# Attention with a routed FFN on one core: another order of the beginning, an earlier z load, larger merge groups and another order of the last FFNs

## The chip, the core and the metric

One core of a Trainium2 chip runs the whole program. The engines are TensorE (PE; its weight loads are PEld), VectorE (DVE), ScalarE (ACT), GpSimd (POOL) and SyncE (SP), which issues nearly all transfers. Each runs its own instructions in the order in which they are written, and waits where an input or a buffer is not free. The metric is the device time of one execution in microseconds, lower is better.

## The reference

Batch 8, sequence 3136, model width 256, width of z 64, FFN width 1024, capacity 128:

```python
scores = (1 / S) * np.matmul(z, z.transpose(0, 2, 1))
attn = np.maximum(scores, 0.0) ** 2
x = u * np.matmul(attn, v)
# then, for each batch b
scores = x[b] @ w_gate
top_idx = np.argpartition(-scores, capacity)[:capacity]
xe = x[b, top_idx]
ye = np.maximum(xe @ w1, 0.0) @ w2
out[b] = x[b]
out[b, top_idx] = xe + sigmoid(scores[top_idx])[:, None] * ye
```

All of it is in float32. The kernel writes each float32 operand of a matmul as a high part (rounded to float32r) and a low part (the rest), and adds the products that matter.

## The kernel before

**Tiles and slots.** The 3136 columns of a batch are cut into seven chunks, 0 to 6: five of 512 and the last two of 256 and 320. The rows are cut into 24 blocks of 128 and one of 64. A slot is one chunk with a pair of row blocks (the last slot of a chunk has the block of 64 alone), so a chunk has 13 slots and a batch 91. For slot k, `scores(k)` multiplies ZH and ZL (high and low part of z) by the chunk's Z tile on PE into one of two score banks; ACT makes relu and its square, which gives the high part `hi`; DVE multiplies score and relu to `a` (L413), or ACT squares again; `low(k)` subtracts for the low part `lo` on POOL or DVE (L459). `mix(k)` multiplies V by hi (8 matmuls) and by lo (4 matmuls) into the accumulators. In the middle of mix(k), at matmul `turn`, the scores of slot k + LEAD (3) are issued. As attn is symmetric, squares of later row blocks are transposed on DVE and stored, and later chunks fetch them (`fetch`, `old_scores`) instead of computing them.

**Preparation.** `stage_z` and `stage_v` issue loads on SP, `prep_z` and `prep_v` split what has landed into high part (ACT) and low part; `bring_z` fills the chunk's Z tile. In `prep_v` the low part is always POOL's. For the batches after the first, z of a whole chunk is loaded into the one `zst` buffer two slots ahead of its `prep_z`, during the batch before.

**Order.** There is one order written out by hand: the loop over slots runs what `plan` holds for the slot, then mix, then the posts of the slot's tasks. What is chosen between engines goes by sums: `spend` adds an estimate to `busy` of an engine, and each slot takes a fixed amount off. `start()` stands ahead of slot 0: ten warm-up matmuls, loads, prep_z of chunk 0, then scores and prep_v for three slots, with prep_z of chunk 1 ahead of the third.

**The routed FFN.** After a batch, `route` and `choose` find the 128 best tokens and `expert` runs the FFN. Two batches' FFNs (5 and 6, in `held`) are put off to the end. In the last batch the choice is made from chunks 0 to 2, and `merge(b, c)` then merges chunks 3 to 6 into it one by one: the scores of the chunk are spread into rows (`spread`, `seen`), `keep_old` and `rank_old` rank the old choice, `count_old` and `count_new` count who beats whom (DVE, L827 and L829), `pick` makes a one-hot matrix and `what`, and `find` multiplies them on PE (L888). `keep_choice` then keeps the new choice for the next merge. A task is a list of PE operations that are placed in the mix of a slot, a post that follows, and a number of slots that the next task has to wait; a task without PE operations may go with the one before it into a slot. What is left after the last slot is run in a final list, with `held` and the last batch's FFN.

Of the kernel before, what the change touches and what calls it, by code (L numbers as in the profile page):

```python
# [40 lines left out]
def constants(S, cap):  # L41
# [25 lines left out]
    for i, (c0, w) in enumerate(chunks_of(S)[-LATE:]):  # L67
        t = c0 + w // 4 * np.arange(4)[None, :] + np.arange(P)[:, None]
        tok[:, i, :, 0] = t // Q * Q
        tok[:, i, :, 1] = t % Q  # L70
# [10 lines left out]
def attention_then_routed_ffn(ctx: ExitStack, tc: tile.TileContext, zt, ut, v, wg, w1, w2, cst, cst16, keys, outs, at, cap):  # L81
# [129 lines left out]
    def stage_z(b, i, n=None):  # L211
# [6 lines left out]
        for h in range(2):  # L218
            nc.sync.dma_start(st[h * 64 : h * 64 + 64, :n], zt[b, :, a : a + n])
        staged["z", b, i] = st  # L220

# [13 lines left out]
    def bring_z(b, c):  # L235
# [3 lines left out]
        for rows, z in ((slice(0, 64), ZH), (slice(64, P), ZL)):  # L239
            if b == 0 and c == 0:  # L240
                nc.scalar.copy(t[rows], z[rows, c0 : c0 + w].bitcast(F32))
# [11 lines left out]
    def stage_v(b, g):  # L253

        st = stage.tile([P, GT, D], F32, name="vst", tag="vst")
        if g < NJ // GT:
            for f in range(GT):
                src = v[b, g * CH + f * P : g * CH + (f + 1) * P, :].rearrange("(t a) d -> a t d", a=Q)
                nc.sync.dma_start(st[f * Q : (f + 1) * Q], src)
# [5 lines left out]
    def prep_v(b, g):  # L265
# [8 lines left out]
        split(src, *[t[:, w].rearrange("p h (f i) -> p h f i", i=Q) for w in range(2)], lo_on=nc.gpsimd.tensor_tensor)  # L274
        for q in range(n):
            V[b, 2 * g + q] = t[:, :, :, q * P : (q + 1) * P]
        spend(act=0.6, pool=1.3)
# [190 lines left out]
    def mix(k, beside, between):  # L468
# [14 lines left out]
        else:  # L483
# [7 lines left out]
            if first:  # L491
                todo.sort(key=lambda x: x[0])
        turn = 6 if first else 4 if last or len(slots[min(k + 1, len(slots) - 1)][2]) == 1 else 8
# [86 lines left out]

    def scores_of(b, c, xT):
# [3 lines left out]
        T4 = w // 4  # L585
        row = moe.tile([P, P + CH], F32, name="row", tag="hl", bufs=2)[:, : P + w]
        col = moe.tile([P, 4], F32, name="col", tag="col", bufs=2)[:T4]
# [8 lines left out]
        def seen(q):  # L596
            if q == 0:
                nc.scalar.copy(row[:, P:], bank[0])
            for i in range(2 * q, 2 * q + 2):
                junk = moe.tile([P, P], F32, name="own", tag="diag", bufs=2)[:T4, :T4]  # L600
                nc.vector.scalar_tensor_tensor(
                    junk, bank[0][:T4, i * T4 : (i + 1) * T4], 1.0, consts["ident"][:T4, :T4],
                    op0=ALU.mult, op1=ALU.mult, accum_out=col[:, i : i + 1],
# [210 lines left out]
    def merge(b, c):  # L814
# [5 lines left out]
        T4 = CHUNKS[c][1] // 4  # L820
# [15 lines left out]
        def keep_old():  # L836
            cnt["o"] = moe.tile([P, 3], F32, name="cnt_o", tag="cnt_o")
            cnt["n"] = moe.tile([P, 4, 3], F32, name="cnt_n", tag="cnt_n")
            cnt["rk"] = moe.tile([P, 5], F32, name="rk5", tag="rk5")
# [11 lines left out]
        def count_new(i, q):  # L851
            s, o = col[:, i : i + 1], P + i * T4
            to = cnt["n"][:T4, i]
            if q == 0:
                count(to[:, 0:1], row[:T4, P - n : o], s, ALU.is_ge)
            else:
                count(to[:, 1:2], row[:T4, o:], s, ALU.is_gt)
                count(to[:, 2:3], row[:T4, o : o + T4], s, ALU.is_equal, consts["before"][:T4, :T4])

        def pick():  # L860
            rk = cnt["rk"]
            nc.vector.tensor_reduce(rk[:T4, :4], cnt["n"][:T4], axis=AX.X, op=ALU.add)
# [391 lines left out]
```

## Time and profile before

| | us |
|---|---|
| median of 3 runs | 2184.3 |
| lowest and highest | 2183.02 and 2185.05 |
| the profiled execution | 2176.7 |
| its span, first to last instruction | 2174.4 |

| engine | busy us | share of the span |
|---|---|---|
| PE | 2111.9 | 97% |
| PEld | 1761.7 | 81% |
| DVE | 1532.7 | 70% |
| POOL | 1328.4 | 61% |
| ACT | 1219.2 | 56% |

The mean granted clock of PE over the span is 0.993 of full speed. A row of a timeline gives start, duration, engine, line, operation, output and inputs, how many instructions it merges, and in brackets how long the engine had been idle and what ended that.

### The profile page before, as it was taken

How to read it: one execution, taken by the hardware profiler on the slowest of the kernel's cores; microseconds unless marked ns; L12 is line 12 of the kernel's file. 1: busy time of each engine (PE TensorE's matmuls, PEld its weight loads, DVE VectorE, ACT ScalarE, POOL GpSimd, SP SyncE). 2: the span in 40 equal slices, each digit the busy share in tenths (PEclk: the TensorE clock that was granted, in tenths of full speed). 3: DMA queues.
4: the chain of work that ended last, by engine and by line, in shares of the span. 5: the costliest groups of instructions: out<-in, count | busy, mean ns of one | idle time of the engine just before them, and what ended most of it. 6: DMA issues, size and time to landing. Idle time of an engine off the chain costs nothing. (4 is left out here: it accounts for less than half of the span.)

```text
span 2174.4 us, 31815 instructions
## 1 busy us (share of the span) xinstructions
PE 2111.9 (97%) x10593; PEld 1761.7 (81%) x10593; DVE 1532.7 (70%) x2340; ACT 1219.2 (56%) x1489; POOL 1328.4 (61%) x691
## 2 busy tenths in 40 slices
PE   7899999999999999999999999999999999999987
PEld 5777888888888798887988889887888889887776
DVE  6656678765777667776677756777577775877785
ACT  5555476544765457654576546654466554765432
POOL 5675476664766557664576655865576665766351
PEclk8999999999999999999999999999999999999998
DMA  4779666787767876678767877678777787757850
GB/s 134 199 227 250 196 189 189 189 215 225 199 178 185 226 222 180 186 198 219 217 185 194 198 209 226 179 200 194 226 204 203 180 205 189 205 163 184 215 158 28
DMA packets 432467, 422.25 MB, mean 194 GB/s; under 512 B 150064, under 2 KB 341040, under 8 KB 428592
## 3 DMA queue, kind: packets, MB, share of 16 engines
q1 hardware_dynamic: 431536, 418.13, 70.8%
q0 software_dynamic: 768, 2.10, 0.4%
q8 instruction: 83, 1.36, 0.3%
q14 instruction: 80, 0.66, 0.1%
HBM read 235.29 MB, written 172.23 MB: 187 GB/s over the span
## 5 line engine op out<-in xcount | busy, mean ns | idle before, releaser
L498 PE MATMUL acc<-hi,V 128*128 128x512 f32 (+2 forms) x5376 | 1236.8, 368 | 7.6 <-ACT hi L372 2.7
L459 POOL TENSOR_TENSOR lo<-a,hi 128x1024 fp32r<-128x1024 f32 (+2 forms) x325 | 750.7, 2312 | 637.0 <-DVE a L413 512.0
L498 PEld LDWEIGHTS acc<-hi,V 128*128 128x128 f32 x5376 | 936.5, 189 | 171.1 <-DVE ut L543 7.8
L498 PE MATMUL acc<-lo,V 128*128 128x512 f32 (+2 forms) x2688 | 670.5, 366 | 15.6 <-POOL lo L459 15.3
L402 ACT ACTIVATE a<-sc 128x1024 f32<-128x1024 f32 (+4 forms) x408 | 362.8, 889 | 521.2 <-PE sc L392 405.0
L498 PEld LDWEIGHTS acc<-lo,V 128*128 128x128 f32 x2688 | 473.9, 189 | 104.8 <-POOL lo L459 23.6
L413 DVE TENSOR_TENSOR a<-sc,a 128x1024 f32<-128x1024 f32 (+2 forms) x330 | 335.0, 1015 | 302.4 <-ACT hi L403 270.8
L428 DVE STREAM_TRANSPOSE aT<-a 128x512 f32<-128x512 f32 (+1 forms) x520 | 341.2, 691 | 101.5 <-ACT a L408 56.4
L372 ACT CAST hi<-qk 128x1024 fp32r<-128x1024 f32 (+2 forms) x320 | 274.2, 861 | 242.7 <-PE acc L498 179.3
L403 ACT ACTIVATE hi<-a 128x1024 fp32r<-128x1024 f32 (+4 forms) x408 | 377.3, 925 | 22.1 <-PE acc L498 4.9
L459 DVE TENSOR_TENSOR lo<-qk,hi 128x1024 fp32r<-128x1024 f32 (+2 forms) x222 | 297.7, 1349 | 87.2 <-ACT hi L372 86.0
L392 PE MATMUL sc<-Z,ZL 128*128 128x512 f32 (+2 forms) x760 | 285.2, 379 | 6.7 <-DVE ZL L117 6.6
L392 PE MATMUL sc<-Z,ZH 128*128 128x512 f32 (+2 forms) x760 | 283.0, 376 | 6.9 <-ACT ZH L116 4.0
L459 POOL TENSOR_TENSOR lo<-qk,hi 128x1024 fp32r<-128x1024 f32 (+2 forms) x98 | 186.1, 1902 | 68.5 <-DVE lo L459 22.4
L392 PEld LDWEIGHTS sc<-Z,ZL 128*128 128x128 f32 x760 | 143.2, 188 | 38.8 <-DVE ZL L117 8.8
L392 PEld LDWEIGHTS sc<-Z,ZH 128*128 128x128 f32 x760 | 143.4, 189 | 36.1 <-ACT ZH L116 5.2
L117 POOL TENSOR_TENSOR V<-vst,V 128x512 fp32r<-128x512 f32 x96 | 132.2, 1384 | 33.4 <-ACT V L116 27.5
L563 POOL TENSOR_TENSOR ut<-x,w_run 128x1024 f32<-128x1024 f32 (+2 forms) x52 | 127.6, 2453 | 24.5 <-DVE x L554 22.5
L117 POOL TENSOR_TENSOR ZL<-zst,ZH 128x512 fp32r<-128x512 f32 (+2 forms) x56 | 67.4, 1208 | 36.7 <-ACT ZH L116 36.7
L116 ACT CAST V<-vst 128x512 fp32r<-128x512 f32 x96 | 58.3, 608 | 44.5 <-DMA vst<-in_v 44.5
L408 ACT ACTIVATE a<-a 128x1024 f32<-128x1024 f32 (+1 forms) x78 | 81.7, 1047 | 2.5
L543 DVE SCALAR_TENSOR_TENSOR ut<-acc,ut 128x512 f32<-128x512 f32 (+2 forms) x112 | 64.0, 613 | 9.6 <-PE acc L498 9.3
(138 smaller groups left out, 1050.9 us busy)
## 6 DMA issues: line engine op xcount, KB each, us to landing
squares<-aT SPq DMA_DIRECT2D x160, 512.0 KB, 3.5
qk<-squares SPq DMA_DIRECT2D x320, 256.0 KB, 5.9
squares_narrow<-aT SPq DMA_DIRECT2D x320, 128.0 KB, 3.7
qk<-squares_narrow SPq DMA_DIRECT2D x80, 512.0 KB, 4.9
vst<-in_v SPq DMA_DIRECT2D x192, 128.0 KB, 3.2
ut<-in_ut SPq DMA_DIRECT2D x40, 512.0 KB, 5.5
out<-x SPq DMA_DIRECT2D x160, 128.0 KB, 3.4
squares_own<-aT SPq DMA_DIRECT2D x39, 256.0 KB, 2.1
```

Source lines behind the costliest of these rows:

```text
L117: (lo_on or nc.vector.tensor_tensor)(lo, src, hi.bitcast(F32), op=ALU.subtract)
L372: nc.scalar.copy(by(hi), src)
L392: nc.tensor.matmul(ps[:, q], z[:, j * P : (j + 1) * P], mov, start=start, stop=not start)
L402: nc.scalar.activation(a, ps[:, :n], AF.Relu)
L403: nc.scalar.activation(pieces[0][0](hi), pieces[0][1], AF.Square)
L408: nc.scalar.activation(a, a, AF.Square)
L413: square = lambda: nc.vector.tensor_tensor(a[rows], ps[rows, :n], a[rows], op=ALU.mult)
L428: nc.vector.transpose(to, a[rows, q].rearrange("p (m t a) -> p m t a", t=GT, a=Q))
L459: on.tensor_tensor(view(lo), src, view(hi).bitcast(F32), op=ALU.subtract)
L498: nc.tensor.matmul(ac[h], w, mov, start=first and h not in started, stop=stop)
L543: nc.vector.scalar_tensor_tensor(xT[:, h, :w], acc[b, c][h], SCALE * SCALE, xT[:, h, :w], op0=ALU.mult, op1=ALU.mult)
L563: nc.gpsimd.tensor_tensor(wx, runs, consts["wg_run"].rearrange("p (o r) -> p o r", o=1).broadcast_to([P, NB, RUN]), op=ALU.mult,)
```

## The change

- `start()`: an early one-column copy on ACT; V of the first two slots is loaded by four DMAs that ACT issues; z of chunk 1 is loaded alone, chunks 2 and 3 behind V of the next slots (`more_z`), chunk 4 and the rest in slots 1 and 2. prep_z of chunk 1 stands ahead of all scores. Only slots 0 and 1 are scored ahead of mix(0); slots 2 and 3 are scored in it after three matmuls. The first V is split on DVE alone. Three warm-up matmuls become two.
- `bring_z` of the first chunk fills both halves of Z from the staged z, one by a copy on ACT, one by a subtraction on DVE.
- `prep_v` in the first batch puts the low part on DVE where POOL's sum is higher. V loads from the fourth on go two slots ahead of their use instead of three.
- In the later batches z of the five whole chunks is loaded five slots ahead instead of two.
- `merge` and `scores_of` work by groups of up to 128 tokens instead of a quarter of the chunk: two groups instead of four in chunk 5 (256), three in chunk 6 (320), four as before in chunks 3 and 4. `pick` rests two slots instead of one.
- The final list is in another order: the choice so far and the spread first, then the merge blended with the kept FFNs, with `find` behind them; one kept FFN is finished and the other's low parts are made while the gather runs, and the other's last matmuls and scatter go into the last FFN.

The diff, cut to its core:

```diff
 def bring_z(b, c):
             if b == 0 and c == 0:
-                nc.scalar.copy(t[rows], z[rows, c0 : c0 + w].bitcast(F32))
+                src, to = (by_rows(x, 0, CH)[rows] for x in (z, t))
+                st = staged["z", 0, 0][rows].rearrange("p (f t a) -> p f t a", t=GT, a=Q)
+                if z is ZH:
+                    nc.scalar.copy(to, st)
+                else:
+                    nc.vector.tensor_tensor(to, st, by_rows(ZH, 0, CH)[rows].bitcast(F32), op=ALU.subtract)
...
-    def prep_v(b, g):
+    def prep_v(b, g, on=None):
...
-        split(src, *[...], lo_on=nc.gpsimd.tensor_tensor)
+        lo_on, took = on or nc.gpsimd, {"dve": 1.0} if on else {"act": 0.6, "pool": 1.3}
+        if not on and b == 0 and busy["pool"] + 1.3 > busy["dve"] + 0.6:
+            lo_on, took = nc.vector, {"act": 0.6, "dve": 0.6}
+        split(src, *parts_of, on and on.tensor_copy, lo_on.tensor_tensor)
...
-        spend(act=0.6, pool=1.3)
+        spend(**took)
...
-            if first:
+            if first and (b or c):
                 todo.sort(key=lambda x: x[0])
-        turn = 6 if first else 4 if last or ...
+        turn = (6 if b or c else 3) if first else 4 if last or ...
...
 def merge(b, c):
-        T4 = CHUNKS[c][1] // 4
+        groups = groups_of(CHUNKS[c][1])
+        NG4 = len(groups)
...
-            *[([], [lambda i=i, q=q: count_new(i, q) for q in range(2)]) for i in range(4)],
-            ([], pick, 1),
+            *[([], [lambda i=i, q=q: count_new(i, q) for q in range(2)]) for i in range(NG4)],
+            ([], pick, 2),
             ([find], (lambda: keep_choice(st)) if more else None),
...
-                at_slots(k, lambda b=b, i=i: stage_z(b, i), use, 0.6)
+                at_slots(k, lambda b=b, i=i: stage_z(b, i), use, 0.6, lead=5 if i < WHOLE else 2)
...
 def start():
         warm(10)
         stage_z(0, 0)
-        stage_v(0, 0)
-        stage_z(0, 1, (WHOLE - 1) * CH)
-        stage_z(0, WHOLE, S + 64 - WHOLE * CH)
+        first = moe.tile([P, 1], F32, name="g", tag="g", bufs=2)
+        nc.scalar.copy(first, idle[0][:, :1])
+        stage_v(0, 0, nc.scalar)
+        stage_z(0, 1, (WHOLE - 1) * CH, CH)
+        stage_v(0, 1)
+        more_z(0, 2, 1)
+        more_z(0, 3, 1)
         prep_z(0, 0)
         bring_z(0, 0)
-        stage_v(0, 1)
-        for k in range(LEAD):
-            if k == LEAD - 1:
-                prep_z(0, 1)
-            more_scores(k)
-            settle_scores()
-            prep_v(0, k)
-        warm(3)
+        prep_z(0, 1)
+        more_scores(0)
+        prep_v(0, 0, nc.vector)
+        busy["pool"] = 3.0
+        settle_scores()
+        more_scores(1)
+        prep_v(0, 1)
+        settle_scores()
+        prep_z(0, 2, 1)
+        warm(2)
         stage_v(0, 2)
...
         held.reverse()
-        run(blend(rest, [t for i in (0, 2, 4) for f, _ in held for t in f[i : i + 2]]))
+        run(rest[:2])
+        *rest, find = rest[2:]
+        (f0, s0), (f1, s1) = held
+        run([*blend(rest, [*f0[:2], *f1[:2], *f0[2:4], *f1[2:4], *f0[4:]]), find])
         order.enter_context(tc.manual_schedule())
-        rest = first[:2] + [t for i in (0, 2) for _, f in held for t in f[i : i + 2]] + first[3:] + ffn + more
+        rest = [*first[:2], *f1[4:], *s0, *s1[:2], *first[3:], *ffn, *s1[2:], *more]
     run(rest)
```

## Rows read from the trace of the kernel before

**Rows 1.** Busy time by stretch: us of PE, PEld, DVE, ACT, POOL; PEclk; DMA share, GB/s.
```profile
10.00:20.00 10.00, 2.63 (x5) 1.22 (x5) 6.31 (x4) 4.75 (x7) 5.78 (x3) 0.50 0.44 102
...
40.00:60.00 20.00, 19.48 (x84) 15.29 (x83) 19.28 (x20) 14.64 (x20) 15.85 (x9) 1.00 0.59 176
...
800.00:1200.00 400.00, 396.98 (x1959) 332.09 (x1958) 294.14 (x441) 240.71 (x289) 264.71 (x136) 1.00 0.73 198
...
2120.00:2140.00 20.00, 14.54 (x88) 14.20 (x87) 15.60 (x66) 5.35 (x9) 6.68 (x5) 0.83 0.08 32
```

**Rows 2.** Waits of PE, whole run: us in total, times, longest us.
```profile
PE ids L888 <- DVE what L747: 8.5, 3, 4.4
```

**Rows 3.** Timeline of the beginning: start us, us, engine, operation, idle time and its releaser.
```profile
2.01 2.00 SPq L259 DMA_DIRECT2D vst<-in_v  x4
...
4.54 1.28 ACT L116 ACT_TABLE_LOAD   x1 [4.54 <-DMA zst<-in_zt]
...
5.83 0.62 ACT L116 CAST ZH<-zst 128x512 fp32r<-128x512 f32 x1
...
6.48 0.69 DVE L117 TENSOR_TENSOR ZL<-zst,ZH 128x512 fp32r<-128x512 f32 x1 [5.34 <-ACT ZH L116]
...
10.21 1.06 ACT L403 ACTIVATE hi<-a 128x1024 fp32r<-128x1024 f32 x1
...
11.29 1.23 DVE L413 TENSOR_TENSOR a<-sc,a 128x1024 f32<-128x1024 f32 x1 [4.12 <-ACT hi L403]
...
14.86 0.79 PE L392 MATMUL sc<-Z,ZH 128*128 128x512 f32 x1 [4.04 <-ACT ZH L116]
...
18.99 0.79 PE L392 MATMUL sc<-Z,ZL 128*128 128x512 f32 x1 [3.33 <-DVE ZL L117]
...
32.88 1.98 PE L498 MATMUL acc<-hi,V 128*128 128x512 f32 x8
...
36.56 1.99 PE L498 MATMUL acc<-hi,V 128*128 128x512 f32 x8
```

**Rows 4.** The same timeline: subtractions on DVE, and POOL's work beside one of them.
```profile
14.93 3.45 POOL L117 TENSOR_TENSOR V<-vst,V 128x512 fp32r<-128x512 f32 x2
...
17.19 1.74 DVE L117 TENSOR_TENSOR ZL<-qk,ZH 128x512 fp32r<-128x512 f32 x1
...
41.14 1.18 DVE L459 TENSOR_TENSOR lo<-a,hi 128x1024 fp32r<-128x1024 f32 x1
```

**Rows 5.** Timeline of the second batch and of the third: staged z.
```profile
483.02 1.21 SPq L219 DMA_DIRECT2D zst<-in_zt  x2
...
493.57 0.62 ACT L116 CAST ZH<-zst 128x512 fp32r<-128x512 f32 x1 [7.93 <-DMA zst<-in_zt]
...
496.31 2.14 PE L498 MATMUL acc<-hi,V 128*128 128x512 f32 x8 [1.25 <-ACT hi L403]
...
500.08 1.19 PE L498 MATMUL acc<-lo,V 128*128 128x512 f32 x4 [1.63 <-POOL lo L459]
...
762.14 1.21 PE L498 MATMUL acc<-lo,V 128*128 128x512 f32 x4 [1.66 <-POOL lo L459]
```

**Rows 6.** Timeline of the last 50 us: merges of the last chunks and the FFN.
```profile
2127.05 0.25 PE L888 MATMUL ids<-what,oh 128*128 128x5 bf16 x4 [4.39 <-DVE what L747]
...
2132.89 0.33 DVE L827 TENSOR_SCALAR_CACHE_REDUCE beats<-row,col 64x128 bf16<-64x128 f32 x1
...
2138.06 0.27 DVE L829 SCALAR_TENSOR_TENSOR beats<-row,col,c_sb 64x64 bf16<-64x64 f32 x1
...
2149.46 0.24 DVE L601 SCALAR_TENSOR_TENSOR own<-spread,c_sb 80x80 f32<-80x80 f32 x1 [4.13 <-ACT row L598]
...
2156.75 0.26 PE L888 MATMUL ids<-c,oh 80*128 80x2 bf16 x4
...
2158.90 2.04 PE L1010 MATMUL y<-ZH,hl 128*128 128x256 f32 x16
...
2162.35 0.73 PE L966 MATMUL h<-wh,xh 128*128 128x512 f32 x2 [1.19 <-ACT xh L116]
```

## What I expect of the change

> **What bounds the kernel now.** I read four views in this order: busy time by stretch, the waits of TensorE (PE), the timeline of the first 45 us, the timeline of the last 75 us. From 800 to 1200 us PE is busy 396.98 of 400 us at full clock; from 10 to 20 us it is busy 2.63 us of 10 at a granted clock of 0.50, and from 2120 to 2140 us 14.54 of 20 at 0.83 [rows 1]. So the middle is bound by PE's own matmuls, which this change leaves alone; time is to be had where PE waits: the beginning, single stalls in the middle, and the end. Each of these is a chain through other engines, and I cost each stretch on its own. A microsecond that PE no longer waits counts fully, as what follows is PE's own work.
>
> The beginning: PE waits 4.04 us for ZH of chunk 1 at 14.86 and 3.33 us for its ZL at 18.99, and the eight first matmuls of mix(2) begin at 32.88 [rows 3]. From there a slot takes 36.56 - 32.88 = 3.68 us, PE's pace. mix(2) is therefore my mark: where it stands after the change is the gain of the beginning. The middle: ScalarE (ACT) waits 7.93 us for the staged z at 493.57, and PE then loses 1.63 us at 500.08 for a low part from GpSimd (POOL) [rows 5]. The end: PE waits for `what` of the merge in three places, 8.5 us together [rows 2], one of them 4.39 us at 2127.05 [rows 6]. There the bound is the chain of the merges on VectorE (DVE): each merge needs the choice of the one before.
>
> **Part 1, the beginning.** The activation table is loaded at 4.54, only when z has landed, and takes 1.28; ZH follows at 5.83 [rows 3]. The new one-column copy takes the load to about 1.2 (when the zero tile is written), so ACT is free at 2.6. Then ACT issues the four loads of V(0): no row shows ACT issuing a DMA; SP needs 2.00 us for the same four [rows 3], and I take 0.5 each (0.1 would do no harm, 1.0 would put ZH at 6.6, later than now). So ACT is free at 4.6 and ZH begins there, 1.2 us earlier. ZL is 0.69 on DVE with POOL idle [rows 3]; the other half of Z is a second such subtraction instead of a copy on ACT. Scores of slot 0 begin near 6.7 and end at 7.7.
>
> The row shows the next cast right at the end of the 1.28 us load, with no gap [rows 3]. The Trainium skill (ScalarE: Activation LUTs, What ACT_TABLE_LOAD costs) adds a drain of 1.38 us to each load; by it ACT would be free at 4.0, ZH would begin at 6.0 and the beginning would gain about 1.4 us less.
>
> Then, with the durations of the rows: two ACT passes of about 1.05 each give hi(0) at 9.8; the product on DVE, 1.23, ends at 11.1 [rows 3]; lo(0) is now on DVE, 1.18 with POOL idle [rows 4], and ends at 12.3. hi(1) is ready at 11.9 and its product at 13.5. PE does three matmuls of mix(0) at 10, scores(2) at 11.1 when the first score bank is free, scores(3) at 13.6 when the second is. z of chunk 1 is a load of its own now and prep_z(0,1) stands ahead of all scores, so the waits of 4.04 and 3.33 us go. From 13.6 PE has 4 + 9 + 16 matmuls up to the end of mix(1): at 3.68/16 = 0.23 us each 6.7 us, to 20.3; if the first 3 to 4 us run at the 0.50 clock that the stretch shows now, 22. mix(2) also needs the low half of V(2). Adding up `spend` by the new rule puts V 2, 3, 5, 6, 10, 11 and 12 on DVE, 1, 4, 7, 8 and 9 on POOL, and all lo but lo(0) on POOL. V(2) stands on DVE behind the products and transposes of slots 2 and 3, and ends at 22 to 23. I put mix(2) at 23.4: a gain of 9.5. The lower bound is mix(2) at 27, if every DVE subtraction meets POOL (1.74 instead of 0.69, [rows 4]): gain 6; the upper is 21, full clock and no contention: gain 12. The later V loads (two slots ahead of their use instead of three) cost nothing: SP now waits with them for the buffer anyway, and two slots are 7.4 us; if that cover fails, a slot waits once for a load.
>
> **Part 2, z five slots in advance.** The load at 483.02 stands behind the two weight copies of the slot on SP's queue; the cast waits for it until 493.57 [rows 5]. Three slots more are about 8 to 11 us, which takes the two z DMAs ahead of those copies, at the price of two issues of 0.6 us in front of a store that no one waits for then. The buffer has been free since the chunk before, over seven slots. The same stall of 1.6 to 1.7 us stands in four passes (500.08, 762.14 and two more, at 1024 and 1287), and in the first PE loses another 1.25 at 496.31; in the fifth pass it is 0.2, in the sixth nothing. Sum 1.63 + 1.25 + 3 x 1.66 + 0.2 = 8.1, of which [rows 5] hold the first two passes. I take 7: what the stalls hide may come up next, such as a Z chunk behind the same copies. Bounds: 8.1, and 3 if ACT finds another late input there.
>
> **Part 3, the end.** Two edits meet. `pick` now rests two slots, so one more slot of PE work, about 1.8 us, stands ahead of each find; PE uses its wait for it. But each find of chunks 3 and 4 comes one slot later, so the merge of chunk 5 begins at slot 9 of the last chunk and not 7, and its find falls out of the loop into the final list. I worked this out from the rule that pops tasks: spread_old with count_old, two groups, two groups, pick, rest, find; and the order now (find at the ends of slots 1, 6, 11) follows from it. The DVE chain sets those times, so the finds of chunks 3 and 4 stay where they are, the second at 2127. For chunk 5 the counts of four groups run from 2132.89 to 2138.3 [rows 6], 1.3 us each with what lies between; two groups fewer save 2.6, of which the spread at the end of slot 9 and pick behind the last scaling on DVE take 0.6: gain 2.0. Then the scores of the last chunk: now DVE waits 4.13 us at 2149.46 for the copy that stands on ACT behind two rectifications [rows 6]. In the new order `seen` comes at once, but spread_old then stands behind twelve hidden matmuls on PE, 12 x 0.23 = 2.8 less 0.5 of DVE's own work, a wait of 2.3: gain 1.8. One group fewer there, with wider rows than in chunk 5: 1.5. The find that now runs at 2156.75 would come at about 2151.4.
>
> Behind it, 2156.75 to the first hidden matmul of the last FFN at 2162.35 is 5.6 us [rows 6]. The kept low parts and one scatter now stand in DVE's order before the gate: later by 0.4. The second kept FFN's last eight matmuls, 2.04/16 = 0.13 each [rows 6], stand between hidden and transposes: 1.0, of which PE's short waits give back 0.2. Net gain of the end 5.3 - 1.2 = 4.1; bounds 0 (the saved waits all come back) and 9 (PE stays at full clock, where it is at 0.83 now).
>
> **Sum.** 9.5 + 7 + 4.1 = 20.6 us. The profiled execution took 2176.7, span 2174.4 plus 2.3 around it; so 2156 for that one. The median of the runs shown is 7.6 above it, and the saving is the same: 2184.3 - 20.6 = 2163.7, rounded 2164. The bounds of the parts alone: gains of 9 to 29.
>
> **The rivals.** *The first batch becomes DVE's.* Eight subtractions more stand on DVE. DVE is busy 19.28 of 20 us from 40 to 60 us already [rows 1]. Beside POOL a 128x512 subtraction took 1.74 instead of 0.69: it began at 17.19 while POOL worked on its pair until 18.38, and ended 0.55 us behind it [rows 4]. If each moved one pays 1.74 or more, 8 x 1.74 = 14 us less one lo of 1.18 come to an engine with 0.04 of its time free: the gain of the beginning would be given back by the end of chunk 0, time 2173. A rule speaks for it: the Trainium skill (SBUF — State Buffer, Who interferes with whom) says that a DVE operation with two SBUF inputs and a POOL operation that reads SBUF exclude each other for a whole instruction. Against it: with all lo on POOL, DVE and POOL fall into turns, and LEAD of three slots, 11 us, covers single blocks. Chance 0.15.
>
> *The end doesn't gain.* The find of chunk 5, out of the loop, and the extra eight matmuls cost what the groups save: 2168; if the final list serialises on DVE, 3 us worse still, 2171. Chance 0.15.
>
> *The z load doesn't do what it says*: it lands earlier, but ACT then waits at the same place for another transfer behind the weight copies, as all of them queue there. 2171. Chance 0.08.
>
> *Slower: the clock.* PE begins early but with holes between 8 and 14 us, and stays at 1.2 GHz while DVE feeds it. Every us at the low level on PE's own work costs 0.5 us, so the low stretch would have to last 41 us longer than now to cancel the 20.6, through most of chunk 0; if it lasts to the end of that chunk near 75 us, 25 us are lost and the time is about 2189. Now the clock rises once PE has had unbroken work from 18.99 on, so I give it 0.05.
>
> **How the numbers follow.** The forecast has 0.57; these four have 0.15, 0.15, 0.08 and 0.05 and none is left over for a gain past the bounds. Range 2155 (all parts at their upper bounds) to 2176 (start given back and one more part failing). A measurement of this kernel tells about 0.2%, 4.4 us, from no change. Faster by more: forecast and the first three rivals, less the cases in which two of them meet: 0.89. Within: 0.06. Slower by more: the clock, 0.05.
>
> **What would show it.** Right: mix(2) near 23, scores beginning before 7, no waits for ZH or ZL of chunk 1; ACT's waits for the staged z gone and PE without the 1.66 us stalls; the last find near 2151 in the old count less 16.5. Wrong: a first load on ACT ending past 6; DVE subtractions of 1.7 us in a row in chunk 0 and PE waiting for V's low half; a granted clock of 0.5 beyond 25 us; a find of the last chunk that keeps its distance from the last mix.

## The result and the profile after

| | before | after |
|---|---|---|
| median beside each other, us | 2183.66 (4 runs) | 2152.88 (4 runs, 2149.70 to 2156.27) |
| ratio, 95% interval | | 0.986, 0.9838 to 0.9883 |
| profiled execution, us | 2176.7 | 2153.18 |
| its span, us; mean granted clock | 2174.4; 0.993 | 2151.4; 0.993 |

The change gains 30.8 us by the medians; 20.6 were forecast, and 2152.88 lies 2.1 us below the lower end of the range. The two profiled executions are only 23.5 us apart: the one of before lies 7.0 us below its median, the one of after 0.3 above. These 7.3 us are most of the 10.2 by which the forecast missed on the medians.

Where the 23 us of span lie, I read with marks: a mark is the begin of the first scaling of the accumulators on DVE (`ut<-acc`, L543 before, L559 after) at the end of a chunk. (7,4) is the mark at the end of chunk 4 of the last batch; "chunk 4 lost" sums, over batches 1 to 5, what chunk 4 takes beyond 36.06 us, its length in every kernel with the early load.

| stretch, us | before | after | gain |
|---|---|---|---|
| to the end of chunk 0 of batch 0 | 80.09 | 70.25 | 9.8 |
| rest of batch 0 | 214.88 | 211.80 | 3.1 |
| chunk 4 of batches 1 to 5, lost | 10.56 | 0.04 | 10.5 |
| the other chunks up to (7,4) | 1589.65 | 1587.58 | 2.1 |
| from (7,4) to the last instruction | 98.92 | 101.43 | -2.5 |

These are one execution of each. In after_again (below) the changed kernel has 70.04, 216.30, 0.04, 1586.69 and 100.90 in the same rows: the gains of chunk 0 and of chunk 4 come again, the 3.1 us of the rest of batch 0 do not.

The beginning, timeline of after, which answers to [rows 3]: start us, us, engine, operation, idle time and its releaser.

```profile
0.74 1.28 ACT L1178 ACT_TABLE_LOAD   x1 [0.74 <-PEq L1284]
1.18 0.88 ACTq L271 DMA_DIRECT2D vst<-in_v  x2
2.03 0.19 ACT L1178 CAST g<-zero 128x1 f32<-128x1 bf16 x1
3.87 2.72 ACTq L271 DMA_DIRECT2D vst<-in_v  x2
6.63 0.62 ACT L116 CAST ZH<-zst 128x512 fp32r<-128x512 f32 x1 [4.40 <-DMA qk<-in_zt]
8.82 0.76 PE L408 MATMUL sc<-Z,ZH 128*128 128x512 f32 x1 [3.18 <-DVE Z L253]
23.09 2.48 DVE L444 STREAM_TRANSPOSE aT<-a 128x512 f32<-128x512 f32 x4
23.52 0.39 PE L514 MATMUL acc<-hi,V 128*128 128x512 f32 x1
25.50 1.34 DVE L117 TENSOR_TENSOR V<-vst,V 128x512 fp32r<-128x512 f32 x2
26.29 2.82 PE L514 MATMUL acc<-hi,V 128*128 128x512 f32 x7 [2.38 <-DVE V L117]
```

The row at 3.87 merges two issues. A timeline that begins at 4.30 shows the second alone:

```profile
6.27 0.32 ACTq L271 DMA_DIRECT2D vst<-in_v  x1
```

The table is loaded at once, and the four issues on ACT last only 0.32 to 0.46 us each. But ACT waits ahead of the third and of the fourth, and ZH begins at 6.63, later than before. In the trace each of the two takes up the semaphore that told of the landing of an earlier load of z, and begins when that load has landed: the third 0.03 us after the first load of chunk 0 (3.84), the fourth 0.02 us after the first load of chunk 1 (6.25). mix(2) has its first matmul at 23.52 and goes on only at 26.29, because V's low part stands on DVE behind four transposes. In between there are no long holes: PE is busy 8.61 of 10 us from 10 to 20 us, against 2.63 [rows 1].

```profile
10.00:20.00 10.00, 8.61 (x30) 5.60 (x29) 6.69 (x7) 7.34 (x9) 4.39 (x3) 1.00 0.32 84
20.00:30.00 10.00, 7.62 (x27) 5.79 (x27) 7.93 (x11) 5.96 (x8) 5.70 (x3) 0.85 0.53 164
```

(Stretches of after: us of PE, PEld, DVE, ACT, POOL; granted clock; DMA share, GB/s.)

The 1.00 of the first row does not fit after's own matmuls: until 12.4 a score matmul lasts 0.63 us, from 14.66 on 0.40. In after_again the 0.63 us stand beside a granted clock of 0.50, so I take it that the first 3.6 us of PE's own work ran at the lower level in after too.

```profile
11.51 0.63 PE L408 MATMUL sc<-Z,ZH 128*128 128x512 f32 x1
14.66 0.40 PE L408 MATMUL sc<-Z,ZL 128*128 128x512 f32 x1
```
```profile
10.33 0.63 PE L408 MATMUL sc<-Z,ZH 128*128 128x512 f32 x1
10.00:12.00 2.00, 2.00 (x6) 1.24 (x4) 1.12 (x2) 1.40 (x2) 0.00 (x0) 0.50 0.58 135
```

(First after, then after_again. From 27 to 30 us the granted clock of after is 0.50 again.)

The middle, which answers to [rows 5]: the waits of PE over the whole run, in us, times, longest, first of before and then of after.

```profile
PE acc L498 <- POOL lo L459: 15.3, 16, 2.5
PE acc L498 <- DVE hi L462: 3.8, 3, 3.5
PE acc L498 <- ACT hi L372: 2.7, 3, 1.4
PE acc L498 <- ACT hi L403: 1.2, 1, 1.2
```
```profile
PE acc L514 <- POOL lo L475: 7.2, 12, 1.9
PE ids L916 <- DVE what L770: 6.3, 3, 3.7
PE acc L514 <- DVE V L117: 2.4, 1, 2.4
```

PE's waits for POOL's low parts halve, ACT no longer waits for a staged z of a later batch (before 41.9 us in 12 waits), and the 3.45 us that PE waited for `hi` at 75.50, the end of chunk 0, are gone.

The end of after, which answers to [rows 2, 6], in its timeline:

```profile
2109.14 0.75 PE L514 MATMUL acc<-hi,Vr 128*128 128x320 f32 x4
2113.58 0.21 PE L916 MATMUL ids<-what,oh 128*128 128x5 bf16 x2 [3.69 <-DVE what L770]
2113.68 2.48 PE L614 MATMUL spread<-ut,w_row 128*128 128x320 f32 x4
2115.49 1.52 PE L994 MATMUL h<-wh,xh 128*128 128x512 f32 x2
2128.99 0.31 PE L916 MATMUL ids<-c,oh 128*128 128x2 bf16 x3
2134.97 0.72 PE L994 MATMUL h<-wh,xh 128*128 128x512 f32 x2 [1.81 <-ACT xh L116]
2137.47 1.22 PE L994 MATMUL h<-wh,xh 128*128 128x512 f32 x2 [0.75 <-ACT hr L1004]
2140.20 1.91 PE L1038 MATMUL y<-ZH,hl 128*128 128x256 f32 x8
```

The find of chunk 5 now stands behind the last mix, in the open: PE waits 3.69 us there, and its next work runs at half speed.

### The profile page after: what moved, and what is told of

The parts are those of the page before. It is cut to its first block, busy times and chain, and to the rows that moved or that the text cites. A ratio compares the mean times of both kernels' runs of the same rounds, so it can differ in the third digit from the quotient of the medians.

```text
span 2151.4 us, 31785 instructions
## 1 busy us (share of the span) xinstructions
PE 2111.1 (98%) x10589; PEld 1766.0 (82%) x10589; DVE 1536.6 (71%) x2327; ACT 1220.0 (57%) x1488; POOL 1326.7 (62%) x684
## 4 chain that ended last, share of the span: by engine, by line
PE 82%; DMA 5%; DVE 4%; issue 3%; ACT 3%; POOL 2%; SPq 1%; POOLq 0%; DVEq 0%; ACTq 0%
PE acc L514 66%; PE sc L408 13%; POOL lo L475 2%; ACT a L418 1%; DVE a L429 1%; ACT hi L419 1%; DMA qk<-squares 1%; DMA squares_narrow<-aT 1%; PE h L994 1%; DMA vst<-in_w 1%; DMA wl<-w2l_there 1%; PE y L1038 1%; DMA vst<-in_v 0%; DVE beats L851 0%; DMA ut<-in_ut 0%
## 5 line engine op out<-in xcount | busy, mean ns | idle before, releaser
L429 DVE TENSOR_TENSOR a<-sc,a 128x1024 f32<-128x1024 f32 (+3 forms) x330 | 334.6, 1014 | 278.1 <-ACT hi L419 244.7
L117 POOL TENSOR_TENSOR V<-vst,V 128x512 fp32r<-128x512 f32 x89 | 122.5, 1380 | 48.3 <-ACT V L116 46.2
L559 DVE SCALAR_TENSOR_TENSOR ut<-acc,ut 128x512 f32<-128x512 f32 (+2 forms) x112 | 64.1, 613 | 19.2 <-PE acc L514 19.0
L117 POOL TENSOR_TENSOR ZL<-zst,ZH 128x512 fp32r<-128x512 f32 (+2 forms) x56 | 73.0, 1309 | 3.2 <-ACT ZH L116 2.8
```

The costliest lines, as they stand in the source:

```text
L117: (lo_on or nc.vector.tensor_tensor)(lo, src, hi.bitcast(F32), op=ALU.subtract)
L429: square = lambda: nc.vector.tensor_tensor(a[rows], ps[rows, :n], a[rows], op=ALU.mult)
L559: nc.vector.scalar_tensor_tensor(xT[:, h, :w], acc[b, c][h], SCALE * SCALE, xT[:, h, :w], op0=ALU.mult, op1=ALU.mult)
```

## The experiments

My theory after the result: the parts add up, the beginning is worth what was forecast, z more than twice its forecast, the end nothing. The rival: the parts help each other (a shorter beginning moves the stalls of z), so that their sum is less than the whole.

**The kernel itself, and each part alone.** after_again is the changed kernel, unedited. start_only keeps of the diff what concerns batch 0's beginning, tail_only what concerns merge groups and the order of the last FFNs, z_only the number of slots (`lead`) by which z is loaded ahead, set in this line:

```diff
-                at_slots(k, lambda b=b, i=i: stage_z(b, i), use, 0.6)
+                at_slots(k, lambda b=b, i=i: stage_z(b, i), use, 0.6, lead=5 if i < WHOLE else 2)
```

> The changed kernel itself, beside the kernel before on one chip. Theory A: the two profiled executions (2176.7 and 2153.2 us) show the whole difference, and the medians 30.8 us apart hold some 7 us of spread between executions of the kernel before; then the difference in alternating runs is 23 to 26 us. Rival B: a timed execution of the kernel before really takes some 7 us more than the profiled one, and the difference is 29 to 32 us.

> The kernel before with the beginning of the changed one alone (loads, order of start, split of the first V, bring_z of the first chunk, V low halves by the sums, V loads two slots ahead, z of the first batch). Theory: the marks at the ends of the chunks show 9.8 us gained by the end of the first chunk and 13 by the end of the first batch, so 11 to 14 us faster. Rival: the gain of the beginning needs the earlier z load of the second batch, which runs in the first, and then it is 9 to 10 us.

> The kernel before with z of the next batch loaded five slots ahead instead of two, nothing else. Theory: the steps at the fifth chunk of batches 1 to 5 (3.5, 2.3, 2.1, 2.1, 0.5 us) are all its work: 9 to 11 us faster, and no waits of ScalarE for the staged z. Forecast of the prediction: 7. Rival: the waits move to another transfer behind the weight copies, under 4 us faster.

> The kernel before with the groups of 128, the rest of two slots behind pick and the new final order, nothing else. Theory from the two traces: from the scaling of the fourth last chunk (2075.48 and 2049.97 us) to the end of the span the changed kernel takes 101.4 us against 98.9, so 2 to 3 us slower. The prediction: 4.1 us faster. Rival: the end is the same and the difference is due to what came before, within 1 us.

| kernel | median, us | gain on 2182.51 of before | ratio, 95% interval |
|---|---|---|---|
| after_again | 2151.39 | 31.1 | 0.9854 (0.9829 to 0.9880) |
| start_only | 2170.47 | 12.0 | 0.9938 (0.9914 to 0.9961) |
| z_only | 2164.72 | 17.8 | 0.9917 (0.9894 to 0.9940) |
| tail_only | 2181.07 | 1.4 | 0.9998 (0.9983 to 1.0014) |

The 31.1 us of after_again are what its rival B gave. The parts add up to 31.2, so the rival that they help each other falls, as far as these medians tell: each ratio is known to 3 to 5 us. z_only's 17.8 lies above everything that was expected of it, and tail_only is neither 4.1 us faster nor 2 to 3 slower. The mis-sized term is z: 17.8 against 7. By the marks z_only is 15.5 us ahead of before at (7,4).

**Which of the early loads counts.** z_i3 loads only the fourth chunk of the next batch's z early (cast in chunk 4, where I had counted the stalls), z_not3 only the other four. The lines with `lead`, here and for z_lead3, stand in the place of z_only's.

```diff
 z_i3
-    lead=5 if i < WHOLE else 2)
+    lead=5 if i == 3 else 2)
 z_not3
+    lead=5 if i < WHOLE and i != 3 else 2)
```

> The kernel before with one edit: of the next batch's z only the fourth chunk (index 3, cast in chunk 4) is loaded five slots ahead, the others two as before. Theory A (the five early loads gave 17.8 us; the stalls in chunk 4 are the larger part, and other chunks hold the rest): 9 to 12 us faster than before, chunk 4 of each pass at 36.05 us, and about 5 us still lost in chunks 5 and 6. Theory B (the whole gain lies in chunk 4, with what follows from it): 16 to 18 us faster.

> The kernel before with one edit: of the next batch's z the chunks 0, 1, 2 and 4 are loaded five slots ahead, the fourth (index 3) two as before. Theory A: 5 to 8 us faster than before, with chunk 4 still 37 to 39.5 us in five passes. Theory B: no more than 2 us faster.

z_i3: 2173.31 us, 9.5 less than the 2182.8 of before, ratio 0.9964 (0.9952 to 0.9975), and chunk 4 loses 0.05 us in all. z_not3: 2175.28 us, 7.5 less, ratio 0.9960 (0.9945 to 0.9975), and chunk 4 loses 10.55. Together 17.0, about the 17.8 of all five: theory A. Nearly half of the gain lies where I had counted no stall. ACT's waits for the staged z show the split, z_i3 first:

```profile
ACT ZH L116 <- DMA zst<-in_zt: 8.8, 6, 3.1
```
```profile
ACT ZH L116 <- DMA zst<-in_zt: 32.6, 5, 8.1
```

**What holds z back.** z_lead3 takes three slots instead of five, z_act leaves the two slots and lets ACT issue the loads.

```diff
 z_lead3
+    lead=3 if i < WHOLE else 2)
 z_act
-    def stage_z(b, i, n=None):
+    def stage_z(b, i, n=None, queue=nc.sync):
-            nc.sync.dma_start(st[...], zt[...])
+            queue.dma_start(st[...], zt[...])
...
+    stage_z(b, i, None, nc.scalar if i < WHOLE else nc.sync)
```

> The kernel before with one edit: the five whole chunks of the next batch's z are loaded three slots ahead instead of two. Theory (z is held by the two weight copies that are issued in front of it in its slot, and by the 2 to 3 us that one slot lasts): one slot earlier puts it in front of them, ScalarE's waits for the staged z in chunk 4 shrink from 8 us to under 3 us, and most of the gain is there, 12 to 17 us. Rival (it is the whole queue, with stores and loads of every slot): one slot gives about a third, 5 to 7 us.

> The kernel before with one edit: the five whole chunks of the next batch's z are issued by ScalarE in the same slot as before (two ahead), not by SP. Theory (what holds z is the line of transfers on SP's queue, 9.3 us from issue to use at 483): on a queue of its own z lands in 2 to 4 us, ScalarE's waits for it go, and 10 to 17 us are gained, less two issues of 0.5 to 1.4 us on ScalarE for each chunk. Rival (the 16 DMA engines are shared by all queues and full of the weight copies' packets): z lands as late as before and the time is within 4 us of before.

z_lead3: 2184.63 us, ratio 1.0017 (1.0003 to 1.0032): nothing is gained, theory and rival both fall. Its timeline of SP's issues says why: the order is the one of before.

```profile
484.10 0.73 SPq L181 DMA_DIRECT2D wh<-w1h_there  x1
484.88 1.55 SPq L181 DMA_DIRECT2D wl<-w1l_there  x1
486.53 1.54 SPq L219 DMA_DIRECT2D zst<-in_zt  x2
...
497.06 0.62 ACT L116 CAST ZH<-zst 128x512 fp32r<-128x512 f32 x1 [8.14 <-DMA zst<-in_zt]
```

z is still issued right behind the two weight copies (of 1 MB each), and the cast begins 10.5 us after its issue. In before, too, z lands 0.6 to 1.3 us behind the second copy, in the four passes for which the trace has both landings. z_act: 2171.18 us, 11.6 less than before, ratio 0.9954 (0.9939 to 0.9970); chunk 4 loses 0.02 us. In its timeline:

```profile
480.20 0.47 ACTq L219 DMA_DIRECT2D zst<-in_zt  x1
480.70 0.63 ACTq L219 DMA_DIRECT2D zst<-in_zt  x1
485.84 0.62 ACT L116 CAST ZH<-zst 128x512 fp32r<-128x512 f32 x1
```

Issued by ACT, z is there at most 5.6 us after its issue, and the cast waits for nothing. In z_act the copies also come later on SP (488.24), so z has both another queue and none of them in front; but as it lies two slots ahead as before, what cost the time is the place behind the copies, not the two slots. Whether z on its own queue would be held by copies under way (the rival) this run does not show: in all five passes they are issued only when z has landed. And without the copies in front SP's queue is only 1 to 2 us slower: these loads land 5.8 to 6.9 us after their issue in z_only, 3.7 to 5.2 in z_act.

**Before, again, and z_not3, again.** No edit. The first three ask whether the profiled execution of before is a usual one, the last where the four other loads pay.

> The kernel before, once more under the profile, to see where its executions differ (2174 to 2191 us). Theory: the early z load is worth 17.8 us in medians against 10.5 us of steps in the trace, because the profiled execution was a mild one; in an execution of 2180 us or more the losses at chunk 4 and chunk 6 of the batches are larger than in the trace known so far (12 to 18 us in all). Rival: the extra time lies in the beginning or the end of the execution.

> The same kernel once more, for a second such trace. Theory: what separates its time from 2176.7 us is found in steps of 2 to 4 us at the chunks of the batches where transfers land late, not in the beginning or the end. Rival: the beginning (first batch) or the end differ by as much as the whole.

> The kernel before itself, once more profiled. Theory: what a usual execution has over the profiled one of 2176.7 us lies in two places, the end (from the last but two chunks on 100 to 104 us instead of 98.9) and single stalls of 1 to 3 us in chunks 1 to 3 and 5 to 6 of the batches; chunk 4 of batches 1 to 5 loses 8 to 11 us in all as in the other profiles.

> The kernel before with the loads of z chunks 0, 1, 2 and 4 five slots ahead, once more profiled. Theory: an execution near its median of 2175.3 or below shows 3 to 8 us less than the kernel before outside chunk 4 (batch 0 behind chunk 0, and chunks 5 to 6 of the others), and the same 8 to 11 us lost in chunk 4. Rival: no place outside chunk 4 differs, and the difference is in the end alone.

| stretch, us | before | before_a | before_b | before_c |
|---|---|---|---|---|
| the execution | 2176.7 | 2182.97 | 2177.33 | 2186.43 |
| to the end of chunk 0 | 80.09 | 79.89 | 79.87 | 80.79 |
| rest of batch 0 | 214.88 | 215.77 | 215.77 | 217.01 |
| chunk 4 lost | 10.56 | 10.25 | 8.43 | 12.02 |
| from (7,4) to the end | 98.92 | 103.65 | 99.31 | 101.76 |

The theory that a usual execution loses much more at z falls: chunk 4 loses 8.4 to 12.0 us in all four. What the longer ones have more is spread out: before_a 4.7 of its 6.2 us behind (7,4); before_b is no longer than before and tells nothing; before_c has 2.8 there, 2.8 in batch 0, 1.5 in chunk 4, and 2.6 spread over the other chunks. z_not3_again took 2178.16 us. It and z_not3 are surely shorter than before in two places alone, chunk 5 of batch 0 (21.17 in both, before 22.23 to 22.52) and of batch 6 (20.30 and 20.29, before 21.48 to 21.82): 2.2 to 2.9 us together. The profiles of all kernels give chunk 6 of batches 3 and 5 as well. Chunk 5 of batches 0 and 6 and chunk 6 of batches 3 and 5 together take 106.5 to 109.3 us (mean 107.4) in the eight without the four other early loads, 103.4 and 103.5 in z_not3 and z_not3_again, and 102.1 to 104.1 (mean 102.9) in the nine with all five. So some 4 of the 7.5 us of the four other loads have a place; where the rest lies stays open.

**The first V's issue.**

```diff
-        stage_v(0, 0, nc.scalar)
+        stage_v(0, 0)
```

> The changed kernel with one edit: the four first loads of V are issued by SP, behind the loads of z of chunk 0, as in the kernel before, and not by ACT. Theory (the ACT-issued loads share the transfers with z of chunk 0 and hold ACT until 6.6 us): z lands near 4.5 us, the first ZH begins at 4.6 to 5.0 instead of 6.63, the first scores begin 1.5 to 2 us earlier than 8.82, and the time falls by 1 to 2 us. Rival (z of chunk 1, which then stands behind four more issues on SP, lands 2 us later and sets the beginning): ZH begins early but the scores of slots 2 and 3 or mix(2) wait longer, and the time is the same within 1 us or worse.

```profile
2.01 2.00 SPq L271 DMA_DIRECT2D vst<-in_v  x4
4.21 0.62 ACT L116 CAST ZH<-zst 128x512 fp32r<-128x512 f32 x1 [1.98 <-DMA zst<-in_zt]
6.40 0.47 PE L408 MATMUL sc<-Z,ZH 128*128 128x512 f32 x1 [1.06 <-DVE Z L253]
23.99 1.89 PE L514 MATMUL acc<-hi,V 128*128 128x512 f32 x7 [0.64 <-DVE V L117]
```

ZH comes 2.4 us earlier, the rest of mix(2) 2.3, the end of chunk 0 3.6 (66.66). Yet the time is 2151.97 us, ratio 0.9852 (0.9839 to 0.9866), that of the changed kernel: by the end of chunk 3 the lead is 0.5 us on after, 4.0 on after_again. The cause held; a gain of 1 to 2 us the medians can't tell from none.

**The low parts of V on POOL alone.**

```diff
-        if not on and b == 0 and busy["pool"] + 1.3 > busy["dve"] + 0.6:
+        if False:
```

> The changed kernel with one edit: in the first batch the low part of V is always made on GpSimd (POOL), save the first, which stays on VectorE (DVE). Theory (the wait of 2.38 us in front of the second half of mix(2) is DVE's queue, where the subtraction stands behind four transposes): that wait goes and the middle of mix(2) comes 1 to 2 us earlier, chunk 0 ends 1 to 2 us earlier. Rival (POOL has less time to give than DVE in chunk 0, which is why the change moved the low parts): the low parts of hi pile up on POOL, PE waits for them in chunk 0, and 2 to 5 us are lost.

2155.14 us, ratio 0.9870 (0.9855 to 0.9885). PE's wait at mix(2) is now 3.53 us, for POOL, where it was 2.38 for DVE, and chunk 0 ends 2.1 us later: the rival, in this place. For chunk 0, moving the low parts to DVE was right; in the median the loss is not clear of the noise.

**The end: rest, bank, order.** rest_one lets `pick` rest one slot; y_bank puts one part of y in another PSUM bank, kept_back finishes both kept FFNs first; rest_one_kept is rest_one with kept_back.

```diff
 rest_one
-            ([], pick, 2),
+            ([], pick, 1),
 y_bank
-            if name == "h" or (not lent and name == "y"):
+            if name == "h":
-            if lent:
+            if lent or name == "y":
 kept_back
-        rest = [*first[:2], *f1[4:], *s0, *s1[:2], *first[3:], *ffn, *s1[2:], *more]
+        rest = [*first[:2], *f1[4:], *s0, *s1, *first[3:], *ffn, *more]
```

> The changed kernel with one edit: pick of a merge rests one slot again instead of two, all else of the change kept. Theory (the rest is what pushed a merge out of the loop): the find of chunk 5 comes back into the loop, at a slot before the last of chunk 6, the final list starts with the spread of chunk 6 and no longer with a wait of 3.7 us for the find of chunk 5; the last find comes 3 to 5 us nearer to the last mix, and the median is 2147 to 2149 against about 2152 for the changed kernel, ratio to the kernel before near 0.984. Rival (PE waits for the choice wherever the find stands, as the merges on VectorE are one chain): PE's three waits for `what` add up to 8 us or more again, chunk 6 becomes 3 to 5 us longer, and the median stays within 2 us of the changed kernel.

> The changed kernel with one edit: the kept FFN of batch 5 puts its y into the accumulator banks instead of one of the two score banks. Theory: in the changed kernel that y, kept until behind the last FFN's hidden matmuls, holds a score bank, so the second hidden half waits 0.75 us for the first one's rectification, PE falls to 1.2 GHz from 2137 to 2143.6 us, and that costs some 3 us; with the bank free the time from the last find to the end is 3 to 4 us shorter than in the changed kernel (22.4 us there). Rival: the eight matmuls between hidden and transposes are the cost, and the bank changes under 1 us.

> The changed kernel with one edit: both kept FFNs are finished ahead of the last FFN, as in the kernel before; nothing of them goes into it. Theory of the bank: 3 to 4.5 us less from the last find to the end than in the changed kernel (the wait, the low clock, and 1 us of matmuls between hidden and transposes). Rival: one more scaling on VectorE ahead of the gate gives back 0.5 us and the gain is under 1.5 us.

> The changed kernel with two edits: pick rests one slot, and both kept FFNs are finished ahead of the last batch's FFN. Theory: the gain of the shorter rest (3 to 5 us) stands, and the finishing order adds nothing (it was 0.5 us against the changed kernel), so 2147 to 2149. Rival: what the shorter rest gives in the loop is lost in the final list, 2151 to 2154.

| kernel | median, us | ratio, 95% interval | (7,4) to the end, us |
|---|---|---|---|
| rest_one | 2155.44 | 0.9876 (0.9861 to 0.9891) | 96.27 |
| y_bank | 2154.10 | 0.9875 (0.9856 to 0.9894) | 98.57 |
| kept_back | 2152.67 | 0.9872 (0.9852 to 0.9892) | 99.39 |
| rest_one_kept | 2153.20 | 0.9858 (0.9843 to 0.9873) | 100.19 |

None is measurably better than the changed kernel, and the 2147 to 2149 us of rest_one and rest_one_kept did not come. In rest_one the find of chunk 5 is back in the loop, as the theory said, and its one profiled execution has the shortest end of all. Its timeline:

```profile
2104.11 0.24 PE L916 MATMUL ids<-what,oh 128*128 128x5 bf16 x4 [1.83 <-DVE what L770]
2113.06 0.20 PE L916 MATMUL ids<-what,oh 128*128 128x5 bf16 x2 [1.02 <-DVE what L770]
2116.04 1.34 PE L614 MATMUL spread<-ut,w_row 128*128 128x320 f32 x4
```

But that execution is its fastest by 4.9 us (the others took 2155.06 to 2156.86). rest_one_kept has the same loop, and there PE waits 4.40 us for the find of chunk 4:

```profile
2106.82 0.25 PE L916 MATMUL ids<-what,oh 128*128 128x5 bf16 x4 [4.40 <-DVE what L770]
```

The three waits for `what` are 5.4 us in rest_one, 6.3 in after and 7.9 in rest_one_kept: this fits a chain of merges on DVE that keeps them, where the order only says which find shows them, but no run takes the chain itself away. The bank theory falls as well: in y_bank the wait of 0.75 us in the last FFN is gone, the low clock comes all the same (2140.3 to 2143.6), and the time stays.

## Why the prediction was right or wrong

**The beginning: right in size (9.5; 9.8 in the marks, 12.0 alone), but not by my steps, and so in part by luck.** The table load came at 0.74, and the next operation on ACT follows 0.01 us behind its end (2.03), as [rows 3] had let expect. The 1.38 us of drain that the Trainium skill adds (ScalarE: Activation LUTs, What ACT_TABLE_LOAD costs) did not show, nor at the second load (484.83 to 486.11, the next operation at 486.13). The step that failed is a wait that I had put at nothing: ACT's issues took less than my 0.5 us each, 0.32 to 0.46, but ACT waited between them until loads of z had landed, and ZH began at 6.63 instead of 4.6, the scores at 8.82 instead of 6.7. v_by_sp shows that it was ACT's issues that held ZH: without them it begins at 4.21. The lower clock that I had allowed 3 to 4 us for came, from 8.8 to 12.4. So PE was done with mix(1) 1.5 to 3 us later than my 20.3 to 22; as I had let mix(2) wait until 23.4 for V(2)'s low part, its first matmul stands at 23.52 all the same. Its other seven came 2.8 us later, as that low part ended at 26.23 and not at 22 to 23, behind DVE's four transposes. The rest of the gain I had not seen at all: PE's wait of 3.45 us for `hi` at the end of chunk 0 went too.

**z: the size was wrong (7; 17.8 measured alone), the mechanism right in chunk 4.** ACT's waits went, no other input took their place, and chunk 4 has its full speed. Two terms failed. First, I summed single stalls that I had found on a timeline, 8.1 us in one chunk, and rounded them down for what might come up next; the chunk's own lengths say 10.5 us, as a pass with a stall is 0.4 to 0.7 us longer than its waits show (38.39 against 36.06 in batch 2, with one wait of 1.66). Nothing came up next. Second, I looked for stalls only where ACT's wait was long and put the four other loads at nothing; alone they gave 7.5 us (z_not3). The view that groups PE's waits held more: 15.3 us for POOL's low parts, of which 5.5 are left in z_only.

```profile
PE acc L498 <- POOL lo L459: 5.5, 11, 1.5
```

The waits for `hi` from L372 (2.7 us) and L403 (1.2) are not among z_only's at all. So three rows of before, 15.3 + 2.7 + 1.2 = 19.2 us, were the upper bound to take instead of 8.1; with it the range would have reached 11 us further down and held the result. Of the 19.2 z_only takes away 13.7, near the 15.5 of its marks. That three slots more are enough was right; z_lead3 shows that one is not.

**The median: a step that failed.** I wrote that the profiled execution lies 7.6 us below the median and that the saving is the same. The changed kernel has no such distance (0.3 us the other way here, 4.7 the other way in after_again). Beside one another before's executions reach from 2174.13 to 2191.5 us, those of z_only from 2162.67 to 2167.51, as if the stalls removed were also what made one execution longer than another; but there are 6 of these against 17, and start_only, with the late load, lies between 2166.19 and 2173.78, so this is an indication and not shown. On the profiled pair the forecast is 2.9 us off (20.6 against 23.5), on the medians 10.2. How much of before's distance is z's and how much is the end's (98.9 to 103.7 us in four profiles), the runs do not settle.

**The end: wrong (4.1; 1.4 alone, within 0.2% of nothing).** The rival that the end doesn't gain held. The count of tasks was right: the find of chunk 5 fell out of the loop. I let the time of the earlier finds stand and costed the move at nothing; in after PE waits 3.69 us for it in the open, and the clock falls (0.57 from 2112 to 2120, 1.00 in rest_one): the four spread matmuls take 2.48 us instead of the 1.34 of rest_one, and the hidden ones up to 2119.35 some 1.8 us more. In this pair the last find came only 2.3 us earlier, counted from (7,4) (81.27 before, 79.02 after), not 5.3. But the pair is not a usual one, as the profiles of all kernels with one of the two ends show:

| end | profiles | (7,4) to the last find, us | last find to the end, us |
|---|---|---|---|
| of before | 11 | 81.3 to 86.0, mean 83.1 | 17.6 to 17.8 |
| of after | 5 | 76.5 to 79.7, mean 78.2 | 21.2 to 22.6, mean 22.0 |

In the mean the last find comes 4.8 us earlier, near the forecast 5.3. The term that failed is the one behind it: I had put 1.2 us there, and it is 3.4 to 5.0 in every one of the five, which eats the gain. Of the 4.8 of the pair (17.65 before, 22.41 after) 2.3 are the new order (19.92 in rest_one, whose final order is the same and whose clock there is that of before, 0.96) and 2.5 the clock, which fell in after and not in rest_one:

```profile
2136.00:2144.00 8.00, 7.20 (x28) 5.85 (x27) 0.87 (x2) 2.10 (x4) 0.99 (x1) 0.57 0.00 0
```
```profile
2135.40:2143.40 8.00, 7.01 (x49) 6.02 (x48) 1.77 (x3) 2.27 (x4) 0.99 (x1) 1.00 0.05 16
```

(Both stretches begin 7 us behind the last find; PE does 28 matmuls in the first, after's, and 49 in the second, rest_one's.) From (7,4) on PE is idle less, 20.1 us instead of 21.4, but busy 81.33 instead of 77.48 us with 524 matmuls instead of 527, at a granted clock of 0.89 instead of 0.92: in this pair waits are saved and clock is lost. Behind the last find the clock falls in all seven profiles in which `pick` rests two slots, for 3.4 to 6.9 us (6.8 in after, 3.4 in after_again), and in neither of the two in which it rests one. PE's waits there are the same in after and rest_one (1.81 and 0.75, 1.80 and 0.75 us), so what ahead of them makes the difference is not shown.

**The other rivals.** DVE did not become the bound of the first batch: PE's one wait for a part of V from DVE is the 2.38 us at mix(2). But the block that the rival went by is there, in after's timeline as in [rows 4]:

```profile
15.61 1.26 POOL L117 TENSOR_TENSOR V<-vst,V 128x512 fp32r<-128x512 f32 x1 [15.16 <-ACT V L116]
16.58 0.84 DVE L117 TENSOR_TENSOR ZL<-qk,ZH 128x512 fp32r<-128x512 f32 x1
...
34.33 2.41 POOL L475 TENSOR_TENSOR lo<-a,hi 128x1024 fp32r<-128x1024 f32 x1 [1.99 <-DVE a L429]
35.45 1.84 DVE L117 TENSOR_TENSOR V<-vst,V 128x512 fp32r<-128x512 f32 x1
```

Both subtractions begin while POOL works and end 0.55 us behind its operation (16.87 and 17.42; 36.74 and 37.29), as the one of [rows 4] did. How long one takes depends on how much of POOL's operation is left. This agrees with the rule of the Trainium skill (SBUF — State Buffer, Who interferes with whom) that the two shut each other out for a whole instruction. What the rival had wrong is the number: of the seven moved subtractions three took 1.70 to 2.26 us, the others 0.43 to 0.73, together 8.3 us and not 14; pool_low shows that for chunk 0 the other choice is worse. Nor did the lower clock last: it ended at about 12.4 us and came back, up to the end of chunk 0, only from 27 to 30. That the time would fall by more than 0.2% was right.

## What to carry to other kernels

Size a stall by the row that groups all waits of the bound engine, and by the length of the same chunk with and without it, not by the stalls found on a timeline. A saving read from one execution holds for the median only if the change leaves alone what scatters; where the profiled execution lies below the median, let the range take in that distance. Work that is taken out of a loop into a serial tail is not free: price its wait there, what stands behind it, and the clock. And take such a tail from several profiles: one pair put the last find 2.3 us earlier, sixteen profiles 4.8.

## What the runs showed of the hardware

- An issue of a DMA lasted 0.32 to 0.46 us on ACT and 0.43 to 0.58 on SP at the beginning (four each, in after and in before). What held ACT to 6.59 in after were two waits between its issues, which ended 0.03 and 0.02 us after earlier loads had landed.
- A load of 128 KB in SP's line behind two copies of 1 MB was used 10.5 us after its issue. Without them in front it landed in 3.7 to 5.2 us, issued by ACT (z_act), and in 5.8 to 6.9, issued by SP (z_only).
- The three DVE subtractions shown that began while POOL worked (17.19 in before, 16.58 and 35.45 in after) each ended 0.55 us behind POOL's operation, and took 1.74, 0.84 and 1.84 us instead of 0.69.
- With the same waits of PE in the same 8 us of the last FFN the granted clock was 0.57 in after and 1.00 in rest_one; in two executions of the changed kernel it stayed low there for 6.8 and for 3.4 us.
